# Attention and mixture of experts in fp32 on one core: sums of w1 kept in memory between two Strassen blocks, sums of w2 on GpSimd one visit ahead

## The chip, the cores and the metric

One core of a Trainium2 chip runs the whole kernel. The metric is device time in microseconds (us); lower is better. The engines are named as the profile names them: PE is TensorE (matmuls; PEld its weight loads), DVE is VectorE, ACT is ScalarE, POOL is GpSimd, SP is SyncE, which here issues nearly all transfers. SBUF is the on-chip memory that all engines read and write, PSUM the one that PE writes.

## The reference, cut to what matters

```python
def attention(q, k, v, omega):            # 4 batches, 8 heads, 576 tokens, 64 columns
    def phi(x): h = x @ omega.T - sum(x*x)/2; return exp(h - max(h)) / sqrt(128)
    q_p, k_p = phi(q * D**-0.25), phi(k * D**-0.25)
    return (q_p @ (k_p.T @ v)) / (q_p @ sum(k_p) + 1e-6)

x = attention(...).transpose(0, 2, 1, 3).reshape(2304, 512)
p = domain_probs / domain_probs.sum(-1)
for e in range(4):                        # w1[e]: 512 x 1024, w2[e]: 1024 x 512
    out += p[:, e:e+1] * (maximum(x @ w1[e], 0) @ w2[e])
```

## The kernel before

Every expert is cut in two halves of its 1024 hidden columns, which gives eight (expert, half) pairs. A *visit* works on one pair for one stretch of token rows: it makes the hidden rows (product with w1, relu), then the output rows (product with w2, scaled by the probability and added into `acc`). Visits 0 to 10 take the first 512 rows, while the attention of the later rows is worked off in between. Visits 11 to 18 (`u == 1`, the first Strassen block) take the next 896 rows for each of the eight pairs, and visits 19 to 26 (`u == 2`, the second block) the last 896 rows for the same eight pairs in the same order. The function of both blocks is `fast`.

All products are fp32 split in two fp32r parts (names ending in h or a for the high part, l for the low part): ACT copies the high part, POOL subtracts it for the low part (`split`, lines 491 and 494), and PE multiplies high by high, high by low and low by high. The product with w1 is Strassen-like, with seven products (`p1` to `p7`) in place of eight. Three of them use quarters of w1 as they are (`w1ah`, `w1al`, made by `direct`) and four use sums of quarters (`w1sh`, `w1sl`): `add` forms those sums in place in the raw tile `w1r` (lines 587 to 590, four instructions for each of two tiles), and `summed` splits them. `sides(v + 1)` makes all this for the next visit in six steps, each taken by a `next(ready)`.

In visits 19 to 25 (`DEEP`) the product with w2 uses seven products as well (`sevens`). It needs sums of rows of the hidden tiles (`t1`, `t2`, `r11`, split into `t_hl`) and sums of w2: `w2_sides` forms them in the tile `w2f` (`sums_of`, lines 539 to 542, four instructions for each of two halves of w2) and splits them into `w2s`. It is driven by `prepare()` inside the same visit; only its first step runs at the end of the visit before.

Instructions stand on each engine in the order in which the code emits them; each engine works in that order and waits at semaphores. A deep visit on PE is: eleven products of `p1` to `p6` (line 797, 448 columns), two groups of the first seventh, `p7(1)`, the third group, `p3(1)`, `p4(1)`, and then the remaining sevenths (line 861, 256 columns): sums 5, block (1, 0), the plain outputs of the fourth tile (lines 639 to 641), sums 6, block (1, 1), sums 7 and the last one. Each group of sevenths goes into half of a PSUM bank that DVE's `gather` (line 656) has read before.

Buffers: two each of `w1r`, `w1ah`, `w1al`, `w1sh`, `w1sl`; three of `w2r`; four of `w2h` and `w2l`; one of `w2f`. SP issues the loads of `w1r` and `w2r` when the buffer that each replaces has been read.

Of the kernel before, what the change touches and what calls it, by code (L numbers as in the profile page):

```python
# [6 lines left out]
F32 = mybir.dt.float32  # L7
# [7 lines left out]
def attention_moe(ctx, tc, kT, qT, kd, qd, kn, qn, vn, omT, probs, w1, w2, out):  # L15
# [10 lines left out]
    nc = tc.nc  # L26
# [15 lines left out]
    att = ctx.enter_context(tc.tile_pool(name="att", bufs=2))  # L42
    moe = ctx.enter_context(tc.tile_pool(name="moe", bufs=1))
    xs = ctx.enter_context(tc.tile_pool(name="xs", bufs=1))
    psum = ctx.enter_context(tc.tile_pool(name="psum", bufs=8, space=bass.MemoryType.PSUM))

    raw_x = xs.tile([P, NP, RING], F32, tag="raw_x", name="raw_x")
# [485 lines left out]
    def w2_sides(v, B):  # L533

        def sums_of(f):
            S = att.tile([P, 2, DM], F32, tag="k", name="w2f", bufs=1)
            (b11, b12), (b21, b22) = ((raw[v, "w2", c][:, :H], raw[v, "w2", c][:, H:]) for c in (f, 2 + f))
            (s2, s3), (s4, s1) = ((S[:, i, :H], S[:, i, H:]) for i in range(2))
            nc.vector.tensor_tensor(s1, b12, b22, ALU.add)  # L539
            nc.vector.tensor_tensor(s2, s1, b11, ALU.subtract)  # L540
            nc.vector.tensor_tensor(s3, b11, b12, ALU.subtract)
            nc.vector.tensor_tensor(s4, b21, s2, ALU.subtract)
            return S

        def plain(c):
            W[v, "w2", c] = a, b = pair_of(("w2h", 512), ("w2l", 512))
            split(raw.pop((v, "w2", c)), a, b, nc.scalar, nc.gpsimd)
            load("w2")

        def summed(S, f, i):  # L550
            tags = (("kp", "kp"), ("qp", "qp"), ("qt", "qt"), ("qth1", "qtl1"))[2 * f + i]
            B[f, i] = a, b = tuple(att.tile([P, DM], F32R, tag=x, name="w2s", bufs=1 if f * i else 2) for x in tags)
            split(S[:, i], a, b, nc.scalar, nc.gpsimd)

        S = sums_of(0)
        yield
        plain(0)
        yield
        summed(S, 0, 0)
        yield  # L560
        summed(S, 0, 1)
        yield
        plain(2)
        yield
        S = sums_of(1)
        plain(1)
        yield
        summed(S, 1, 0)
        yield
        summed(S, 1, 1)  # L570
        yield
        plain(3)
        yield

    def sides(v):

        tiles = [raw.pop((v, "w1", i)) for i in range(2)]
        A, S = {}, {}

        def direct(i):  # L580
            A[i] = ah, al = pair_of(("w1ah", 3 * H), ("w1al", 3 * H))
            for r, cs in ((tiles[i][:, :2 * H], slice(0, 2 * H)), (tiles[i][:, 3 * H:], slice(2 * H, 3 * H))):
                split(r, ah[:, cs], al[:, cs], nc.scalar, nc.gpsimd)

        def add(i):
            r11, r12, r21, r22 = (tiles[i][:, j * H:(j + 1) * H] for j in range(4))
            nc.vector.tensor_tensor(r22, r21, r22, ALU.add)  # L587
            nc.vector.tensor_tensor(r21, r11, r21, ALU.subtract)  # L588
            nc.vector.tensor_tensor(r11, r22, r11, ALU.subtract)
            nc.vector.tensor_tensor(r12, r12, r11, ALU.subtract)  # L590

        def summed(i):
            S[i] = sh, sl = pair_of(("w1sh", 4 * H), ("w1sl", 4 * H))
            split(tiles[i], sh, sl, nc.scalar, nc.gpsimd)
            W[v, "w1", i] = {
                p: tuple(x[:, j * H:(j + 1) * H] for x in t)
                for t, at in ((A[i], (1, 2, 4)), (S[i], (6, 3, 7, 5)))
                for j, p in enumerate(at)
            }
            load("w1")  # L600

        direct(0)
        yield
        direct(1)
        yield
        add(0)
        yield
        summed(0)
        yield
        add(1)  # L610
        yield
        summed(1)
        yield

# [134 lines left out]
    def start_sides2(v):  # L749
        B = {}  # L750
        g = w2_sides(v, B)
        next(g)
        sides2[v] = B, g

    def fast(v):

        u, n = visits[v][0], BIG // 2
# [7 lines left out]
        if deep:  # L765
            if v == DEEP[0]:
                sevens_t.append(xs.tile([P, 7, 2, WT], F32R, tag="raw_x", name="t_hl"))
                start_sides2(v)
            B, ready2 = sides2.pop(v)
            T = {p: (sevens_t[0][:, i], sevens_t[0][:, i + 1]) for p, i in ((5, 0), (6, 2), (7, 4))}  # L770
            t1, t2 = (x.rearrange("p t c -> p (t c)")[:, :2 * WT].rearrange("p (k x) -> p k x", k=2) for x in (va, vb))
            r11 = att.tile([P, 2, WT], F32, tag="q", name="r11", bufs=1)

        def prepare():
            if deep:
                next(ready2, None)
            else:
                split_w2()

# [83 lines left out]
        def sevens():  # L863

            L, R, QS3 = slice(0, H), slice(H, DM), range(3)

            def block(g, j):
                return [tuple(x[:, j * FH * P:j * FH * P + WT] for x in hs[2 * g + f]) for f in range(2)]

            def sums_of(i):  # L870
                return [tuple(x[:, f] for x in T[i]) for f in range(2)]

            def weights(g, cs):
                return [tuple(x[:, cs] for x in W[v, "w2", 2 * g + f]) for f in range(2)]

            def mixed(i, cs):
                return [tuple(x[:, cs] for x in B[f, i]) for f in range(2)]

            X, Z = [], []
            for q in QS3[:2]:  # L880
                X.append(bank("g2"))
                seventh(q, X[q][:, L], block(0, 0), weights(0, L))
            p7(1)
            less(t2[:, 1], last_rows(P_[1]["p5"]), t1[:, 1])
            X.append(bank("g2"))
            seventh(2, X[2][:, L], block(0, 0), weights(0, L))
            p3(1)
            less(t2[:, 0], last_rows(P_[1]["u2"]), t1[:, 0])
            p4(1)
            nc.gpsimd.tensor_tensor(r11, t2, r11, ALU.subtract)  # L890
            nc.scalar.activation(T[6][0], t2, AF.Copy)
            less(t1[:, 1], first_rows(P_[1]["u"]), t2[:, 1])
            for q in QS3:
                gather(v, X[q][:, L], q, L)
            nc.vector.tensor_tensor(T[6][1], t2, f32(T[6][0]), ALU.subtract)
            less(t1[:, 0], first_rows(P_[1]["p1"]), t2[:, 0])
            next(ready, None)
            split(r11, *T[7], nc.scalar, nc.gpsimd)
            for f in range(2):
                split(t1[:, f], *(x[:, FH * P:] for x in hs[f]), nc.scalar, nc.gpsimd)  # L900
            next(ready, None)
            yield 1
            for q in QS3:
                seventh(q, X[q][:, R], sums_of(5), mixed(1, R), start=False)
            yield 1
            zs = []
            for q in QS3:
                if q < 2:
                    Z.append(bank("g2"))
                zs.append(Z[q // 2][:, q % 2 * H:(q % 2 + 1) * H])  # L910
                seventh(q, zs[q], block(1, 0), weights(1, L))
            for q in QS3:
                gather(v, zs[q], q, L)
            next(ready, None)
            yield 1
            ps = bank("g2")
            outputs(v, hs, ps, 3, range(FH))
            gather(v, ps, 3)
            next(ready, None)
            yield 1  # L920
            for q in QS3:
                seventh(q, X[q][:, L], sums_of(6), mixed(0, L), start=False)
                gather(v, X[q], 4 + q)
            yield 1
            next(ready, None)
            for q in QS3:
                seventh(q, X[q][:, R], block(1, 1), mixed(1, L), start=False)
                gather(v, X[q][:, R], 4 + q, L)
            next(ready, None)
            yield 1  # L930
            for q in QS3:
                seventh(q, X[q][:, L], sums_of(7), mixed(0, R), start=False)
                gather(v, X[q][:, L], 4 + q, R)
            if v + 1 in DEEP:
                start_sides2(v + 1)
            yield 1
            for q in QS3:
                seventh(q, X[q][:, L], [tuple(x[:, FH * P:] for x in hs[f]) for f in range(2)], weights(1, R), start=False)
                gather(v, X[q][:, L], q, R)
            for t in range(tiles):  # L940
                gathered(v, t)
            yield 1
# [29 lines left out]
        if deep:  # L972
            nc.scalar.activation(r11[:, 1], first_rows(P_[0]["u"]), AF.Relu)
            less(t1[:, 1], last_rows(P_[0]["p5"]), r11[:, 1])
            p6(1)
            split(t1, *T[5], nc.scalar, nc.gpsimd)
            yield from sevens()
            return
        prepare()
# [309 lines left out]
```

## Time and profile before

| what | value |
|---|---|
| runs shown, median | 994.41 us (992.71 to 996.43, 3 runs) |
| the profiled execution's own time | 998.48 us |
| its span, from first to last instruction | 996.4 us |
| PE busy | 925.0 us (93%), 5286 matmuls |
| DVE, ACT, POOL busy | 653.7, 488.5, 497.9 us |
| moved by DMA | 83.63 MB, read 77.99 MB, written 4.72 MB |

Busy times are sums over the span; an engine that is not the last to be waited for can be idle at no cost. So the table says only that PE is nearest to being full; where PE is not, the views by stretch and by wait say.

### The profile page before, as it was taken

Reading aid. Unit: us, or ns where it says so; the run is one execution under the profiler, and the core shown is the slowest. Engines: PE = TensorE matmul, PEld = TensorE weight load, DVE = VectorE, ACT = ScalarE, POOL = GpSimd, SP = SyncE. Lnnn points to the kernel's source line nnn. Section 1 sums busy time; section 2 is a strip of 40 time slices with the busy share of each in tenths; the row PEclk is TensorE's granted clock in tenths of the full one; section 3 lists DMA queues with packets and bytes.
Section 4 is the critical chain, followed back from the end, with each engine's and each line's share of the span. In section 5 each row is a group of like instructions: output and inputs, shape, how many; then the busy total and the mean of one; then the engine's idle time right before and its main releaser. Section 6 shows DMA issues by size and latency. Waiting matters only on the chain. (4 is left out here: it accounts for less than half of the span.)

```text
span 996.4 us, 14354 instructions
## 1 busy us (share of the span) xinstructions
PE 925.0 (93%) x5286; PEld 816.6 (82%) x5286; DVE 653.7 (66%) x1076; ACT 488.5 (49%) x1092; POOL 497.9 (50%) x387
## 2 busy tenths in 40 slices
PE   9999999999999999999999999797878787878898
PEld 9898888887888888888888888687868686877787
DVE  5654677775685564657657578777676777776753
ACT  6455776776744645354535535454343434343430
POOL 5664565655344443434433344566565656564630
PEclk9999999999899999999999999998999998999899
DMA  7654454534215231312321122311101111202001
GB/s 194 163 185 148 127 162 141 162 124 143 74 53 148 75 98 56 101 43 64 101 64 43 42 64 85 95 43 43 53 32 53 32 53 33 68 19 74 11 11 74
DMA packets 47365, 83.63 MB, mean 84 GB/s; under 512 B 8704, under 2 KB 17088, under 8 KB 47296
## 3 DMA queue, kind: packets, MB, share of 16 engines
q1 hardware_dynamic: 47056, 82.43, 27.2%
q8 instruction: 41, 0.67, 0.3%
q10 hardware_dynamic: 240, 0.30, 0.1%
q14 instruction: 28, 0.23, 0.1%
HBM read 77.99 MB, written 4.72 MB: 83 GB/s over the span
## 5 line engine op out<-in xcount | busy, mean ns | idle before, releaser
L494 POOL TENSOR_TENSOR w2l<-w2r,w2h 128x512 fp32r<-128x512 f32 x93 | 126.4, 1365 | 141.2 <-ACT w2h L491 113.6
L656 DVE SCALAR_TENSOR_TENSOR acc<-g,pr,acc 128x512 f32<-128x512 f32 (+1 forms) x207 | 121.5, 616 | 69.0 <-PE g L641 40.9
L494 POOL TENSOR_TENSOR w1sl<-w1r,w1sh 128x1024 fp32r<-128x1024 f32 (+1 forms) x59 | 112.7, 1911 | 102.6 <-ACT w1sh L491 91.6
L639 PE MATMUL g<-w2h,hh 128*128 128x512 f32 x368 | 147.4, 401 | 0.4 <-ACT hh L843 0.4
L641 PE MATMUL g<-w2h,hl 128*128 128x512 f32 x368 | 144.5, 393 | 0.0
L640 PE MATMUL g<-w2l,hh 128*128 128x512 f32 x368 | 144.2, 392 | 0.0
L494 POOL TENSOR_TENSOR w1al<-w1r,w1ah 128x256 fp32r<-128x256 f32 (+1 forms) x77 | 89.4, 1178 | 53.1 <-ACT w1ah L491 46.3
L814 DVE SCALAR_TENSOR_TENSOR hl<-sum,hh 128x448 fp32r<-128x448 f32 (+1 forms) x96 | 64.3, 670 | 69.6 <-ACT hh L813 69.6
L808 DVE TENSOR_TENSOR sum<-g,sum 128x448 f32<-128x448 f32 x96 | 59.5, 620 | 75.5 <-PE g L797 74.7
L813 ACT ACTIVATE hh<-sum 128x448 fp32r<-128x448 f32 (+1 forms) x96 | 50.8, 529 | 116.6 <-DVE sum L808 116.6
L797 PE MATMUL g<-xbh,w1sh 128*128 128x448 f32 x256 | 94.9, 371 | 3.2 <-ACT sum L803 3.2
L491 ACT ACTIVATE w1sh<-w1r 128x1024 fp32r<-128x1024 f32 (+1 forms) x59 | 51.0, 867 | 95.6 <-DVE w1r L590 95.5
L861 PE MATMUL g<-w2s,t_hl 128*128 128x256 f32 x378 | 64.9, 341 | 33.7 <-ACT w1ah L491 18.7
L797 PE MATMUL g<-xbl,w1sh 128*128 128x448 f32 x256 | 94.2, 368 | 0.0
L797 PE MATMUL g<-xbh,w1sl 128*128 128x448 f32 x256 | 94.0, 367 | 0.0
L861 PEld LDWEIGHTS g<-w2s,t_hl 128*128 128x128 f32 x378 | 61.5, 246 | 38.0 <-ACT w1ah L491 20.8
L803 ACT ACTIVATE sum<-g 128x448 f32<-128x448 f32 x96 | 51.6, 538 | 72.9 <-PE g L797 72.9
L797 PE MATMUL g<-xbh,w1ah 128*128 128x448 f32 x192 | 72.2, 376 | 15.8 <-DVE sum L808 15.8
L641 PEld LDWEIGHTS g<-w2h,hl 128*128 128x128 f32 x368 | 69.4, 188 | 16.2 <-DVE hl L844 0.7
L639 PEld LDWEIGHTS g<-w2h,hh 128*128 128x128 f32 x368 | 69.6, 189 | 14.4 <-ACT hh L843 0.8
L640 PEld LDWEIGHTS g<-w2l,hh 128*128 128x128 f32 x368 | 69.5, 189 | 12.3
L797 PE MATMUL g<-xbh,w1al 128*128 128x448 f32 x192 | 70.9, 369 | 0.0
(195 smaller groups left out, 2234.8 us busy)
## 6 DMA issues: line engine op xcount, KB each, us to landing
w1r<-in_w SPq DMA_DIRECT2D x54, 512.0 KB, 3.6
w2r<-in_w SPq DMA_DIRECT2D x108, 256.0 KB, 2.7
out<-acc SPq DMA_DIRECT2D x18, 256.0 KB, 2.5
va<-in_vn SPq DMA_DIRECT2D x14, 256.0 KB, 4.6
k<-in_kd SPq DMA_DIRECT2D x12, 288.0 KB, 3.2
k<-in_kn SPq DMA_DIRECT2D x12, 288.0 KB, 4.4
q<-in_qd SPq DMA_DIRECT2D x12, 288.0 KB, 4.4
q<-in_qn SPq DMA_DIRECT2D x12, 288.0 KB, 5.0
```

Of the source, the lines that this page charges most:

```text
L491: hi.activation(a, t, AF.Copy)
L494: lo.tensor_tensor(c, t, f32(a), ALU.subtract)
L639: nc.tensor.matmul(ps, ha[:, ts_], wa, start=(c == 0), stop=False)
L640: nc.tensor.matmul(ps, ha[:, ts_], wc, start=False, stop=False)
L641: nc.tensor.matmul(ps, hc[:, ts_], wa, start=False, stop=(c == FH - 1))
L656: nc.vector.scalar_tensor_tensor(acc[i][:, cs], ps, sc, acc[i][:, cs], ALU.mult, ALU.add)
L797: nc.tensor.matmul(ps, a[:, w], x[:, k], start=(start and k + at == 0), stop=(k == 1 and at == 2), skip_group_check=not start)
L803: nc.scalar.activation(t, P_[g][where], AF.Copy)
L808: nc.vector.tensor_tensor(t, P_[g][where], t, ALU.add)
L813: nc.scalar.activation(ha, t, AF.Relu)
L814: nc.vector.scalar_tensor_tensor(hc, t, 0.0, f32(ha), ALU.max, ALU.subtract)
L861: nc.tensor.matmul(to, x, w, start=(start and f + k == 0), stop=(f + k == 3), skip_group_check=not start)
```

## The change

In the first block every visit stores its four tiles of split sums of w1 (high and low part of two tiles, 512 KB each) to memory, at the visit's start, through SP (`keep_sides`). In the second block `sides` leaves out `add` and `summed`: the tiles are loaded back from there by four DMAs that POOL issues (`fetched`), behind the first `direct`. The raw tiles `w1r` are still loaded, for the three quarters that `direct` takes.

The four additions of each `sums_of` of w2 move from DVE to POOL. `w2_sides` has another order of steps, and it starts one visit ahead: the first `sums_of` is emitted before `sevens()`, and both plain parts of the first half and its two summed splits inside `sevens()` of the visit before; `prepare()` does the rest, with a list that says how many steps each call takes.

```diff
@@ w2_sides
-            nc.vector.tensor_tensor(s1, b12, b22, ALU.add)
-            nc.vector.tensor_tensor(s2, s1, b11, ALU.subtract)
-            nc.vector.tensor_tensor(s3, b11, b12, ALU.subtract)
-            nc.vector.tensor_tensor(s4, b21, s2, ALU.subtract)
+            nc.gpsimd.tensor_tensor(s1, b12, b22, ALU.add)
+            nc.gpsimd.tensor_tensor(s2, s1, b11, ALU.subtract)
+            nc.gpsimd.tensor_tensor(s4, b21, s2, ALU.subtract)
+            nc.gpsimd.tensor_tensor(s3, b11, b12, ALU.subtract)
...
+    def keep_sides(v):
+
+        for i in range(2):
+            kept[visits[v][1:3], i] = ts_ = tuple(
+                scratch.tile([P, 4 * H], F32, tag=f"s{visits[v][1:3]}{i}{x}", name="kept", bufs=1) for x in "hl"
+            )
+            for k, t in zip(ts_, made.pop((v, i))):
+                nc.sync.dma_start(k, f32(t))
...
+        def fetched(i):
+            S[i] = pair_of(("w1sh", 4 * H), ("w1sl", 4 * H))
+            for t, k in zip(S[i], kept[visits[v][1:3], i]):
+                nc.gpsimd.dma_start(t, k)
+
+        direct(0)
+        if visits[v][0] < 2:
+            yield
+        else:
             load("w1")
-
-        direct(0)
-        yield
+            fetched(0)
+            parts(0)
+            fetched(1)
+            yield
+            direct(1)
+            load("w1")
+            parts(1)
+            yield
+            return
         direct(1)
...
+            steps2 = [2, 1, 1, 1, 1, 1, 1, 1] if v == DEEP[0] else [1, 1, 1, 0, 0, 1, 1, 0]
...
+        if u == 1:
+            keep_sides(v)
+
         def prepare():
             if deep:
-                next(ready2, None)
+                for _ in range(steps2.pop(0)):
+                    next(ready2, None)
...
             gather(v, ps, 3)
-            next(ready, None)
+            on_sides2(v + 1)
+            on_sides2(v + 1)
             yield 1
...
-            if v + 1 in DEEP:
-                start_sides2(v + 1)
+            on_sides2(v + 1)
             yield 1
...
             split(t1, *T[5], nc.scalar, nc.gpsimd)
+            if v + 1 in DEEP:
+                start_sides2(v + 1)
             yield from sevens()
```

PE has the same instructions in the same order in both kernels. On the other engines the change shows at three places of each deep visit.

The first place is DVE in `sevens`, from the split of t2 (L895, in the change L941) to the gather before the last groups; `acc<-g` are gathers. Before:

```order
L895 TENSOR_TENSOR t_hl<-vb,t_hl 128x768
L781 SCALAR_TENSOR_TENSOR va<-sum,vb 128x384
L656 SCALAR_TENSOR_TENSOR acc<-g_7222,pr,acc 128x256 x2
L656 SCALAR_TENSOR_TENSOR acc<-g_7229,pr,acc 128x256
L587 TENSOR_TENSOR w1r<-w1r 128x256
L588 TENSOR_TENSOR w1r<-w1r 128x256
L589 TENSOR_TENSOR w1r<-w1r 128x256
L590 TENSOR_TENSOR w1r<-w1r 128x256
L656 SCALAR_TENSOR_TENSOR acc<-g_7249,pr,acc 128x512
```

and four gathers on, the same four additions of the second tile. In the change:

```order
L941 TENSOR_TENSOR t_hl<-vb,t_hl 128x768
L827 SCALAR_TENSOR_TENSOR va<-sum,vb 128x384
L693 SCALAR_TENSOR_TENSOR acc<-g_7281,pr,acc 128x256 x2
L693 SCALAR_TENSOR_TENSOR acc<-g_7288,pr,acc 128x256
L693 SCALAR_TENSOR_TENSOR acc<-g_7312,pr,acc 128x512
L693 SCALAR_TENSOR_TENSOR acc<-g_7184,pr,acc 128x512
```

Both sets of additions are gone from between the gathers.

The second place is DVE beside the products `p2` to `p7` of the same visit; `sum<-g` reads a product from PSUM. Before:

```order
L808 TENSOR_TENSOR sum<-g_6995,sum 128x448
L814 SCALAR_TENSOR_TENSOR hl<-sum,hh 128x448
L539 TENSOR_TENSOR w2f<-w2r 128x256
L540 TENSOR_TENSOR w2f<-w2f,w2r 128x256
L541 TENSOR_TENSOR w2f<-w2r 128x256
L542 TENSOR_TENSOR w2f<-w2r,w2f 128x256
L808 TENSOR_TENSOR sum<-g_7057,sum 128x448
L814 SCALAR_TENSOR_TENSOR hl<-sum,hh 128x448
```

In the change:

```order
L854 TENSOR_TENSOR sum<-g_7063,sum 128x448
L860 SCALAR_TENSOR_TENSOR hl<-sum,hh 128x448
L854 TENSOR_TENSOR sum<-g_7113,sum 128x448
L860 SCALAR_TENSOR_TENSOR hl<-sum,hh 128x448
L854 TENSOR_TENSOR sum<-g_7048,sum 128x448
```

The four additions for w2 no longer stand between the read of `p2` and that of the later products.

The third place is POOL around `p4(1)`, from the split of t1 (`t_hl<-va`) on; `r` is r11. Before:

```order
L494 TENSOR_TENSOR t_hl<-va,t_hl 128x768
L890 TENSOR_TENSOR r_7376<-vb,r_7376 128x768
L494 TENSOR_TENSOR w1al<-w1r,w1ah 128x512
L494 TENSOR_TENSOR w1al<-w1r,w1ah 128x256
L494 TENSOR_TENSOR t_hl<-r_7376,t_hl 128x768
L494 TENSOR_TENSOR hl<-va,hh 128x384 x2
L494 TENSOR_TENSOR w1al<-w1r,w1ah 128x512
L494 TENSOR_TENSOR w1al<-w1r,w1ah 128x256
L494 TENSOR_TENSOR w1sl<-w1r,w1sh 128x1024 x2
```

In the change:

```order
L495 TENSOR_TENSOR t_hl<-va,t_hl 128x768
L540 TENSOR_TENSOR w2f<-w2r 128x256
L541 TENSOR_TENSOR w2f<-w2f,w2r 128x256
L542 TENSOR_TENSOR w2f<-w2r,w2f 128x256
L543 TENSOR_TENSOR w2f<-w2r 128x256
L936 TENSOR_TENSOR r_7436<-vb,r_7436 128x768
L495 TENSOR_TENSOR w1al<-w1r,w1ah 128x512
L495 TENSOR_TENSOR w1al<-w1r,w1ah 128x256
L625 DMA w1sh<-kept 128x1024
L625 DMA w1sl<-kept 128x1024
L625 DMA w1sh<-kept 128x1024
L625 DMA w1sl<-kept 128x1024
```

Four additions now stand ahead of `r`, four DMA issues behind the first `w1al`, ahead of `t_hl<-r`; the two `w1sl` of 1024 columns are gone.

On SP the four stores `kept<-w1sh`, `kept<-w1sl` of a visit of the first block stand behind the loads of `w1r` of the visit before and ahead of the visit's four loads of `w2r`.

## Rows read from the trace of the kernel before

**Rows 1.** Busy time by stretch: length, each engine's busy us, granted PE clock, DMA.
```profile
540.00:590.00 50.00, 50.00 (x244) 44.03 (x244) 28.75 (x41) 21.44 (x42) 20.89 (x16) 1.00 0.19 59
741.07:789.33 48.26, 39.15 (x222) 36.11 (x222) 34.71 (x57) 18.59 (x36) 28.21 (x19) 0.93 0.15 44
```

**Rows 2.** What PE waited for from 600 us on: us, times, longest.
```profile
PE g L861 <- ACT w1ah L491: 18.7, 6, 3.1
PE g L797 <- DVE sum L808: 15.8, 7, 3.0
PE g L861 <- DVE acc L656: 15.2, 11, 2.0
PE g L861 <- DVE hl L844: 5.8, 5, 1.2
PE g L861 <- ACT acc L654: 4.0, 2, 2.8
```

**Rows 3.** Timeline of PE, 741 to 790 us: rows with idle time before them.
```profile
742.55 3.87 PE L861 MATMUL g<-w2s,t_hl 128*128 128x256 f32 x18 [3.12 <-ACT w1ah L491]
...
754.16 0.50 PE L861 MATMUL g<-w2s,hh 128*128 128x256 f32 x2 [0.69 <-DVE acc L656]
...
758.55 3.34 PE L861 MATMUL g<-w2s,t_hl 128*128 128x256 f32 x18 [2.00 <-DVE acc L656]
...
777.65 0.47 PE L797 MATMUL g<-xbh,w1ah 128*128 128x448 f32 x1 [2.14 <-DVE sum L808]
...
782.10 0.39 PE L861 MATMUL g<-w2h,hl 128*128 128x256 f32 x1 [1.16 <-DVE hl L844]
```

**Rows 4.** Busy time by stretch, two stretches behind the third stall (columns as 1).
```profile
711.80:715.10 3.30, 3.30 (x18) 3.30 (x17) 2.23 (x6) 0.00 (x0) 1.48 (x1) 0.50 0.19 47
...
950.75:954.05 3.30, 3.30 (x16) 3.30 (x17) 1.48 (x4) 0.42 (x1) 2.38 (x1) 0.50 0.00 0
```

**Rows 5.** Timeline of DVE, 741 to 776 us: additions and what stands behind.
```profile
755.34 1.30 DVE L587 TENSOR_TENSOR w1r<-w1r 128x256 f32<-128x256 f32 x1
...
757.93 1.26 DVE L656 SCALAR_TENSOR_TENSOR acc<-g,pr,acc 128x256 f32<-128x256 f32 x3
...
771.66 1.50 DVE L539 TENSOR_TENSOR w2f<-w2r 128x256 f32<-128x256 f32 x1 [1.66 <-POOL w2s L494]
...
775.18 0.61 DVE L808 TENSOR_TENSOR sum<-g,sum 128x448 f32<-128x448 f32 x1
```

**Rows 6.** Timeline of DVE and POOL, 783 to 790 us.
```profile
785.90 0.62 DVE L814 SCALAR_TENSOR_TENSOR hl<-sum,hh 128x448 fp32r<-128x448 f32 x1 [0.70 <-ACT hh L813]
...
788.72 0.55 DVE L781 SCALAR_TENSOR_TENSOR vb<-sum,va 128x384 f32<-128x384 f32 x1
...
789.41 1.83 POOL L890 TENSOR_TENSOR r<-vb,r 128x768 f32<-128x768 f32 x1 [3.43 <-DVE vb L781]
```

**Rows 7.** Timeline of DVE, 776 to 783 us, beside POOL's w2s.
```profile
778.94 1.34 DVE L781 SCALAR_TENSOR_TENSOR va<-sum,r 128x384 f32<-128x384 f32 x1
```

**Rows 8.** Groups of POOL by shape: busy us, mean ns of one.
```profile
L366 POOL TENSOR_TENSOR raw_x<-nu,dn 128x256 f32<-128x256 f32 x8 | 5.9, 736 | 13.0 <-ACT hh L630 5.4 <-DVE dn L364 3.9 <-ACT sum L491 3.7
```

**Rows 9.** Timeline of POOL, 741 to 763 us, behind the first stall.
```profile
742.95 2.70 POOL L494 TENSOR_TENSOR w1al<-w1r,w1ah 128x512 fp32r<-128x512 f32 x2
745.61 2.16 POOL L494 TENSOR_TENSOR t_hl<-r,t_hl 128x768 fp32r<-128x768 f32 x1
```

**Rows 10.** DMA: issues by line (KB, us to landing), an SP timeline, a busy stretch.
```profile
w1r<-in_w SPq DMA_DIRECT2D x54, 512.0 KB, 3.6
...
28.02 2.39 SPq L124 DMA_DIRECT2D q<-in_qT  x4
...
56.00:60.00 4.00, 4.00 (x35) 3.81 (x33) 2.04 (x8) 1.76 (x5) 2.56 (x2) 1.00 0.98 304
```

**Rows 11.** Timeline of POOL and ACT around visit 18's start, 581 to 598 us.
```profile
581.62 2.40 POOL L494 TENSOR_TENSOR w1sl<-w1r,w1sh 128x1024 fp32r<-128x1024 f32 x1 [2.89 <-ACT w1sh L491]
...
597.23 0.62 ACT L491 ACTIVATE w2h<-w2r 128x512 fp32r<-128x512 f32 x1
```

More of the change, by code (lines that the diff above doesn't have):

```diff
@@ L44, in attention_moe @@
     xs = ctx.enter_context(tc.tile_pool(name="xs", bufs=1))
+    scratch = ctx.enter_context(tc.tile_pool(name="scratch", bufs=1, space=bass.MemoryType.DRAM))
     psum = ctx.enter_context(tc.tile_pool(name="psum", bufs=8, space=bass.MemoryType.PSUM))
@@ L546, in plain @@
             W[v, "w2", c] = a, b = pair_of(("w2h", 512), ("w2l", 512))
-            split(raw.pop((v, "w2", c)), a, b, nc.scalar, nc.gpsimd)
-            load("w2")
+            split(raw[v, "w2", c], a, b, nc.scalar, nc.gpsimd)
         def summed(S, f, i):
@@ L557, in w2_sides @@
         plain(0)
+        load("w2")
+        yield
+        plain(1)
+        yield
+        summed(S, 0, 1)
         yield
@@ L560, in w2_sides @@
         yield
-        summed(S, 0, 1)
+        plain(2)
+        load("w2")
         yield
-        plain(2)
+        plain(3)
         yield
         S = sums_of(1)
-        plain(1)
+        load("w2")
+        load("w2")
+        yield
+        summed(S, 1, 1)
         yield
@@ L569, in w2_sides @@
         yield
-        summed(S, 1, 1)
-        yield
-        plain(3)
-        yield
+    made, kept = {}, {}
+    def keep_sides(v):
[5 more added lines that the diff above has]
+                nc.sync.dma_start(k, f32(t))
     def sides(v):
@@ L594, in summed, with parts @@
             split(tiles[i], sh, sl, nc.scalar, nc.gpsimd)
+            made[v, i] = S[i]
+            parts(i)
+            load("w1")
+        def parts(i):
             W[v, "w1", i] = {
@@ L599, in summed @@
             }
-            load("w1")
-        direct(0)
-        yield
+        def fetched(i):
[4 more added lines that the diff above has]
+        if visits[v][0] < 2:
+            yield
+        else:
+            load("w1")
+            fetched(0)
+            parts(0)
+            fetched(1)
+            yield
+            direct(1)
+            load("w1")
+            parts(1)
+            yield
+            return
         direct(1)
@@ L753, in start_sides2, with on_sides2 @@
         sides2[v] = B, g
+    def on_sides2(v):
+        if v in sides2:
+            next(sides2[v][1])
     def fast(v):
@@ L918, in sevens @@
             gather(v, ps, 3)
-            next(ready, None)
+            on_sides2(v + 1)
+            on_sides2(v + 1)
             yield 1
@@ L924, in sevens @@
             yield 1
-            next(ready, None)
             for q in QS3:
@@ L928, in sevens @@
                 gather(v, X[q][:, R], 4 + q, L)
-            next(ready, None)
+            on_sides2(v + 1)
             yield 1
@@ L933, in sevens @@
                 gather(v, X[q][:, L], 4 + q, R)
-            if v + 1 in DEEP:
-                start_sides2(v + 1)
+            on_sides2(v + 1)
             yield 1
```

## The prediction

> **What bounds the kernel now.** I read the stretches first, to see where PE is not full, then the waits of PE summed by what ended them, then the timeline of one deep visit to find the instruction that is really late, and last the rows of the engines that would get new work.
>
> In the first block PE is busy for the whole 50 us that the first of [rows 1] shows, at full clock, so no faster preparation can shorten it; it can only be disturbed. A deep visit (the second row) is different: it lasts 48.26 us, PE is busy 39.15 of them, and the mean granted clock is 0.93. The 9.1 us without PE lie in five waits, which [rows 3] show for one visit: 3.12 us ahead of sums 5, 0.69 ahead of block (1, 1), 2.00 ahead of sums 7, 2.14 ahead of a product of the next visit and 1.16 ahead of its first sevenths. I call them stalls 1 to 5. [Rows 2] give their sums over the kernel.
>
> What ends each, read from [rows 5] and [rows 6]:
> - Stalls 2 and 3 end with gathers of DVE. The second of them, at 757.93, comes straight behind the additions of w1 that began at 755.34: DVE spent 2.59 us on work that PE does not need for another 20 us.
> - Stall 4 ends with the read of a product at 775.18. Ahead of it stand four additions of w2, from 771.66 on, the first of which had waited 1.66 us for POOL.
> - Stall 5 ends behind DVE operations that ran slowly beside POOL's splits of w2: 1.34 us in [rows 7] for an operation that takes 0.55 in [rows 6].
> - Stall 1 is named a wait for ACT, but what comes last is DVE's gather behind a chain of reads, splits and sums of p7(1) on DVE and ACT. None of it is in the diff, so this stall stays.
>
> The clock is the second loss. [Rows 4] show two stretches right behind stall 3 at a granted 0.50, the 1.2 GHz level, after full speed (2.4 GHz) and a wait; there are five such stretches of about 3.4 us, and the two rows are the first and the last. PE runs without a gap there, so each costs half its length, 1.7 us. The mean of 0.93 in the second of [rows 1] says the same of a visit: 0.07 of 48.26 is 3.4 us, two such losses, one behind stall 3 and one behind stall 1.
>
> **The change part by part.** The sum is made against the profiled execution, 998.48 us, and is scaled to the median, 994.41, at the end.
>
> Taken away. The eight w1 additions and the eight of w2 leave DVE, so stalls 2 to 4 lose their cause, and stall 5 loses it too, since POOL no longer splits w2 there. By [rows 2] that is 15.8 us (DVE sum), 15.2 (DVE acc), 5.8 (DVE hl), and of the 4.0 on ACT acc the part that is not stall 1 of the first deep visit, 4.0 − 2.8 = 1.2: together 38.0 us. The 18.7 us on w1ah are stall 1 of the other visits and stay. Without stall 3 the clock should stay up there: 5 × 1.7 = 8.5 us. Gained: **46.5 us**. From below, a gather waits for its own matmuls as well, and some tenths of each wait may remain: with 0.3 us left in each of these 25 waits it would be 7.5 us less.
>
> Put on POOL, first part: four additions of w2 ahead of r. The nearest row is POOL's 128x256 subtraction, 736 ns [rows 8], so 2.94 us a visit. POOL is idle there, 3.43 us, waiting for DVE's vb at 788.72 [rows 6], so by length they fit. But that idle time is just when DVE works through the chain that ends stall 1, from 785.90 to 789.27, with operations that read two tiles of SBUF, and [rows 7] show such an operation at 1.34 in place of 0.55 beside POOL. The cost lies between zero (the additions fall into DVE's own waits for ACT) and their whole length, 2.94 us a visit. Walking the two lists against each other, with an operation that meets one of POOL's held until that ends, two of the four additions land in DVE's waits for ACT and two hold it, so that vb ends about 1.5 us late (2 × 0.74). I take that. Six visits, 19 to 24, prepare a successor this way: **9.0 us** given back, with 0 and 17.8 as bounds; stall 1 grows from 3.1 to about 4.6 us.
>
> A rule of the Trainium skill speaks against the change here. Its page "SBUF — State Buffer", section "Who interferes with whom", has VectorE and GpSimd share one pair of ports under an exclusive lock: a VectorE operation with two SBUF inputs and a GpSimd operation exclude each other for a whole instruction. The 1.34 against 0.55 agrees with a wait of one instruction. Taken strictly for all four additions, the rule gives the bound of 17.8 us, a time of 967.
>
> The first deep visit has no visit ahead that would prepare it, and all its w2 work for the first half stands on POOL at once. By the same rows that is four low parts, two sums' low parts and the four additions, more than 10 us where 2.94 are new, of which half fits beside other work: **1.5 us** late, from 0 to 2.94.
>
> Put on POOL, second part: four DMA issues a visit, behind the first w1al and ahead of t_hl<-r. No row shows what a DMA issue costs POOL. From below, SP issues four in 2.39 us, 0.6 each; from above, I take the time in which such a transfer lands, 3.6 us, as if POOL were held until then [rows 10]. What waits behind is t_hl<-r, which sums 7 need. In [rows 9] w1al ends at 745.65, 3.1 us after sums 5 begin, and t_hl<-r takes 2.16. Sums 7 begin 758.55 − 742.55 = 16.0 us after sums 5 [rows 3], 13.3 without stalls 2 and 3. So an issue costs nothing up to (13.3 − 3.1 − 2.2) / 4 = 2.0 us, and each us above that costs 4 us a visit, 28 us over seven visits. I take 1.2 us, double SP's, nearer to that row than to the landing: cost **nothing**. In return POOL is rid of two w1sl a visit of 2.4 us each, by the first of [rows 11].
>
> On this the Trainium skill's page "DMA: Bandwidth & Descriptors", section "Latency and other measured facts", puts the first byte at about 1 us from GpSimd and 0.6 from SP. No row here shows the former; as an estimate from that page the four would hold POOL 4 us, and the sum is the same.
>
> The fetched tiles have to be there for the first product with a sum of w1, about 20 us after sums 5 begin. Issued between 3 and 8 us after it, and landing 3.6 us later (twice that if the 2.1 MB share the queues with w1r and w2r), they are there by 15: 5 us of cover, nothing paid.
>
> The stores. In the first block SP issues four of 512 KB per visit ahead of the visit's loads of w2r. They cannot start until w1sl is done, 581.62 + 2.40 = 584.02 for visit 18 [rows 11]; 2.1 MB at the 304 GB/s that a busy stretch moved [rows 10] take 7 us, so w2r is loaded by about 592, and ACT first uses it at 597.23. Cover 5 us, cost nothing; with the cover gone each us would cost up to 8, as PE is full there.
>
> The sum: 998.5 − 46.5 + 9.0 + 1.5 = 962.5 us. The profile lies 4.07 us above the median, so **958 us** (0.963 of before). A steady deep visit should come to 48.3 − 6.0 − 1.7 + 1.5 = 42.1 us.
>
> **The rivals.**
> - *No collision.* If POOL's additions end before DVE reaches its chain, 9 us of the price vanish: 949. For it: DVE's list is shorter ahead of that place, and POOL's sums can start earlier. Against it: 1.34 us in [rows 7]. If beyond that the clock stayed up behind stall 1 as well (6 × 1.7), 939.
> - *Full collision, or POOL late.* All four additions hold DVE (967), or an issue takes about 2.5 us (972). For it: POOL is the engine that gets both new kinds of work.
> - *The change does not deliver.* If stores hold w2r up past its cover, say by 2.5 us in eight visits of the first block, where PE has no slack, or the fetched tiles land as much too late, 20 to 30 us come back: 978 to 988. For it: SP's queue is in order. Against it: DMA is at 59 GB/s there [rows 1].
> - *The other side: the issues hold POOL.* With 3.6 us each, the four take 14.4; t_hl<-r comes 3.1 + 14.4 + 2.2 − 13.3 = 6.4 us late in seven visits: 45 us given back, 1003 us. It breaks even at 3.3 us an issue and is slower by over 0.5% from about 3.5. The skill's page "SBUF — State Buffer", section "SBUF: two separate sides", speaks for it: a DMA from GpSimd has its descriptors written by GpSimd, which VectorE's port use can lock out. No run here shows that yet. Against it: DVE is idle for part of that stretch, since it waits for PE's groups.
>
> **How the numbers follow.** The forecast's own range, 948 to 968, has a chance of 0.50; no collision (below 948) 0.13; full collision or POOL late (968 to 978) 0.18; not delivered (978 to 993) 0.11; POOL held by the issues 0.08. From 940 to 982 about 0.18 is left out: the held POOL, most of the undelivered case and the case with the clock up everywhere. 0.5%, 5 us, is about what a measurement of this kernel can tell from no change. Faster by more than that: all of the first three cases and half of the fourth, 0.87. Slower: most of the last, 0.06. Between: 0.07.
>
> **What would show it.** Stalls 2 to 5 should be gone from the waits of PE, with no more half-clock stretch behind sums 7 and a visit near 42 us. Stall 1 should stand at about 4.6 us, with POOL's additions of w2 beside lengthened DVE operations. Each issue on POOL should take less than 2.0 us, and the first block should keep PE full. If the first block grows, it is the stores; if sums 7 wait for POOL's t_hl, it is the issues; if the products with sums wait for a DMA, it is the fetch.

## The result, and the profile after

The changed kernel takes 948.4 us (median, 947.31 to 950.36) beside 995.26 us for the kernel before: ratio 0.9535, 95% interval 0.9508 to 0.9561. The forecast was 958, with a range of 940 to 982. The profiled execution spans 947.4 us, 49.0 less than before; the sum had 36.0.

Where the time came from: stretches of the profile after, with the columns of [rows 1].

```profile
540.00:590.00 50.00, 50.00 (x245) 44.01 (x244) 28.68 (x41) 21.55 (x42) 20.85 (x16) 1.00 0.34 116
688.15:728.88 40.73, 36.51 (x222) 34.45 (x223) 24.19 (x41) 17.28 (x34) 31.02 (x30) 0.93 0.31 104
```

The first block is as it was, PE busy all 50 us, though DMA moves 116 GB/s there in place of 59. A deep visit has shrunk from 48.3 to 40.7 us. DVE is down from 34.7 to 24.2 us of it, POOL up from 28.2 to 31.0.

The waits of PE from 600 us on, to be held against [rows 2]:

```profile
PE g L907 <- ACT w1ah L492: 24.2, 6, 4.2
PE g L907 <- ACT acc L691: 4.2, 2, 4.0
PE g L907 <- ACT hh L889: 1.8, 1, 1.8
PE g L907 <- DVE hl L890: 0.2, 1, 0.2
```

Stalls 2 to 5 are gone, but for some tenths in the first deep visit. Stall 1 has grown from 3.1 to 4.2 us, and one wait of 1.8 us is new, in the first deep visit. The two engines beside stall 1, DVE first, then POOL, in their timelines from 681 to 695 us:

```profile
682.08 1.25 DVE L860 SCALAR_TENSOR_TENSOR hl<-sum,hh 128x448 fp32r<-128x448 f32 x1 [0.65 <-ACT hh L859]
683.26 1.09 DVE L827 SCALAR_TENSOR_TENSOR vb<-sum,va 128x384 f32<-128x384 f32 x1
...
685.52 0.62 DVE L860 SCALAR_TENSOR_TENSOR hl<-sum,hh 128x448 fp32r<-128x448 f32 x1 [0.64 <-ACT hh L859]
686.06 0.55 DVE L827 SCALAR_TENSOR_TENSOR vb<-sum,va 128x384 f32<-128x384 f32 x1
```

```profile
682.11 0.74 POOL L540 TENSOR_TENSOR w2f<-w2r 128x256 f32<-128x256 f32 x1
682.93 1.00 POOL L541 TENSOR_TENSOR w2f<-w2f,w2r 128x256 f32<-128x256 f32 x1
684.00 0.92 POOL L542 TENSOR_TENSOR w2f<-w2r,w2f 128x256 f32<-128x256 f32 x1
684.89 0.72 POOL L543 TENSOR_TENSOR w2f<-w2r 128x256 f32<-128x256 f32 x1
...
691.14 0.57 POOL L625 DMA_DIRECT2D w1sh<-kept  x1
```

The first hl and vb take 1.25 and 1.09 us; the same two operations two rows down, with POOL past its additions, take 0.62 and 0.55. That is 1.17 us, and stall 1 is 1.1 us longer. Two of POOL's four additions are longer as well, 1.00 and 0.92 for 0.74. A DMA issue holds POOL 0.57 us.

### The profile page after: what moved, and what is told of

Read it like the earlier page. It is cut to its first block, busy times and chain, and to the rows that moved or that the text cites. A ratio compares the mean times of both kernels' runs of the same rounds, so it can differ in the third digit from the quotient of the medians.

```text
span 947.4 us, 14345 instructions
## 1 busy us (share of the span) xinstructions
PE 906.0 (96%) x5286; PEld 804.1 (85%) x5286; DVE 574.4 (61%) x956; ACT 476.2 (50%) x1076; POOL 518.3 (55%) x459
## 5 line engine op out<-in xcount | busy, mean ns | idle before, releaser
L495 POOL TENSOR_TENSOR w2l<-w2r,w2h 128x512 fp32r<-128x512 f32 x93 | 122.4, 1325 | 141.3 <-ACT w2h L492 107.3
L693 DVE SCALAR_TENSOR_TENSOR acc<-g,pr,acc 128x512 f32<-128x512 f32 (+1 forms) x207 | 124.4, 618 | 89.6 <-PE g L678 57.0
L495 POOL TENSOR_TENSOR w1al<-w1r,w1ah 128x256 fp32r<-128x256 f32 (+1 forms) x77 | 87.2, 1151 | 50.1 <-ACT w1ah L492 47.1
L495 POOL TENSOR_TENSOR w1sl<-w1r,w1sh 128x512 fp32r<-128x512 f32 (+1 forms) x43 | 74.9, 1743 | 61.0 <-ACT w1sh L492 52.7
L860 DVE SCALAR_TENSOR_TENSOR hl<-sum,hh 128x448 fp32r<-128x448 f32 (+1 forms) x96 | 59.4, 618 | 73.0 <-ACT hh L859 73.0
L907 PE MATMUL g<-w2s,t_hl 128*128 128x256 f32 x378 | 57.4, 314 | 28.1 <-ACT w1ah L492 24.2
L907 PEld LDWEIGHTS g<-w2s,t_hl 128*128 128x128 f32 x378 | 54.8, 219 | 31.1 <-ACT w1ah L492 26.3
L843 PE MATMUL g<-xbl,w1ah 128*128 128x448 f32 x192 | 70.1, 365 | 0.0
```

The costliest lines, as they stand in the source:

```text
L495: lo.tensor_tensor(c, t, f32(a), ALU.subtract)
L693: nc.vector.scalar_tensor_tensor(acc[i][:, cs], ps, sc, acc[i][:, cs], ALU.mult, ALU.add)
L843: nc.tensor.matmul(ps, a[:, w], x[:, k], start=(start and k + at == 0), stop=(k == 1 and at == 2), skip_group_check=not start)
L860: nc.vector.scalar_tensor_tensor(hc, t, 0.0, f32(ha), ALU.max, ALU.subtract)
L907: nc.tensor.matmul(to, x, w, start=(start and f + k == 0), stop=(f + k == 3), skip_group_check=not start)
```

## The experiments

Each ratio is to the kernel before, run on the same chip. The diffs are against the changed kernel where nothing else is said.

**1. The w1 part alone.** The w2 functions are those of before; the rest is the change.

```diff
-            nc.gpsimd.tensor_tensor(s1, b12, b22, ALU.add)
...
+            nc.vector.tensor_tensor(s1, b12, b22, ALU.add)
...
-            on_sides2(v + 1)
+            if v + 1 in DEEP:
+                start_sides2(v + 1)
```

> The w1 part alone: tiles of split sums stored in the first block and fetched in the second; the additions of w2 stay on DVE, inside their own visit, as before. Theory (each part takes away its own waits): the waits of PE on DVE's gathers (15.2 us and 1.2 us before) go, each with some 0.27 us that the idle rows don't show, and with them the half-clock stretches behind sums 7 (8.5 us); the waits on the product read (15.8 us) and on hl (5.8 us) stay, stall 1 stays at 3.1 us. Span 996.4 - 16.4 - 3.0 - 8.5 = 968 us, ratio to before about 0.972. Rival 1 (one late chain: taking DVE's w1 additions away only makes PE wait longer at the w2 additions): little gain, ratio 0.985 or more. Rival 2 (the w2 additions were late only because POOL was busy with w1sl): the waits on the product read and on hl go too, ratio near 0.95.

Measured: 964.04 us, 0.9685 (0.966 to 0.9709). The waits of PE from 600 us on:

```profile
PE g L901 <- ACT w1ah L492: 18.7, 6, 3.1
PE g L837 <- DVE sum L848: 15.0, 7, 2.2
PE g L901 <- ACT acc L687: 2.8, 1, 2.8
PE g L901 <- DVE hl L884: 2.3, 2, 1.2
```

The theory holds row by row: the gathers' waits are gone, stall 4 and stall 1 stand as in [rows 2]. Rival 2 has a small share, since hl fell from 5.8 to 2.3 us.

**2. The w2 part alone.** The w1 functions are those of before.

```diff
-        if visits[v][0] < 2:
-            yield
-        else:
-            load("w1")
-            fetched(0)
...
-            return
+        yield
...
-            keep_sides(v)
```

> The w2 part alone: additions of w2 on POOL, one visit ahead; the sums of w1 are formed on DVE and split on POOL in every visit, as before. Theory (each part its own waits): the waits on the product read (15.8 us) and on hl (5.8 us) go, with 0.27 us each that no idle row shows (3.2 us), the gathers' waits (16.4 us) and the clock loss behind sums 7 stay, and stall 1 grows by 1.1 us in six visits beside POOL's additions (6.6 us, and 1.2 us in the first deep visit). Span 996.4 - 24.8 + 7.8 = 979 us, ratio about 0.983. Rival (POOL, which keeps two w1sl of 2.4 us each and gets the additions, becomes late): PE waits for POOL's w2s or w2l about 3 us a visit, ratio 1.00 or more.

Measured: 995.0 us, 1.000 (0.9984 to 1.0017): nothing. The rival's number came out, but not by the rival's mechanism. The waits of PE, and DVE's second set of w1 additions with the POOL rows beside it:

```profile
PE g L872 <- ACT w1ah L492: 23.8, 6, 4.2
PE g L872 <- DVE acc L661: 22.1, 7, 3.9
```

```profile
706.28 1.30 DVE L592 TENSOR_TENSOR w1r<-w1r 128x256 f32<-128x256 f32 x1
707.61 1.37 DVE L593 TENSOR_TENSOR w1r<-w1r 128x256 f32<-128x256 f32 x1
709.01 1.37 DVE L594 TENSOR_TENSOR w1r<-w1r 128x256 f32<-128x256 f32 x1
710.41 0.42 DVE L595 TENSOR_TENSOR w1r<-w1r 128x256 f32<-128x256 f32 x1
710.76 1.26 DVE L661 SCALAR_TENSOR_TENSOR acc<-g,pr,acc 128x256 f32<-128x256 f32 x3
```

```profile
704.89 2.40 POOL L495 TENSOR_TENSOR w1sl<-w1r,w1sh 128x1024 fp32r<-128x1024 f32 x1 [2.37 <-ACT w1sh L492]
707.25 2.84 POOL L495 TENSOR_TENSOR w2l<-w2r,w2h 128x512 fp32r<-128x512 f32 x2
```

Stalls 4 and 5 went, as expected. But the two w2l that this part takes one visit ahead land beside DVE's second additions of w1 and stretch the second and third of them to 1.37 us, where an undisturbed one takes 0.42. (The first, 1.30 us, stands beside w1sl and took as long in the kernel before, in [rows 5].) The gather behind them comes 1.9 us later and stall 3 is 3.9 us. Stall 1 pays its 1.1 us too, and a stretch behind it of 5.45 us ran at half clock (741.45 to 746.90, granted 0.50). What the part saves at one end of the visit it loses at the other: PE's waits from 600 us on sum to 56.7 us in place of 61.2, and the mean granted clock, 0.959 in place of 0.968, takes the rest.

**3. The same, with the low parts of w2 back inside the visit** (diff against 2).

```diff
-            steps2 = [2, 1, 1, 1, 1, 1, 1, 1] if v == DEEP[0] else [1, 1, 1, 0, 0, 1, 1, 0]
+            steps2 = [2, 1, 1, 1, 1, 1, 1, 1]
...
-            on_sides2(v + 1)
-            on_sides2(v + 1)
...
```

> The w2 part alone, with the low parts of w2 back inside their own visit: POOL still makes the additions of w2 one visit ahead, but splits none of w2 beside DVE's additions of w1. Theory (the w2 part alone gained nothing because POOL's two w2l, moved one visit ahead, run beside DVE's second four additions of w1 and lengthen three of them from 0.43 to 1.37 us, which takes stall 3 from 2.0 to 3.9 us and prolongs the half clock behind it): stall 3 is back at 2.0 us, 6 x (1.9 + up to 1.7) = 11 to 21 us better than the w2 part alone, ratio to before 0.979 to 0.989. Rival 1 (stall 3 grew for another reason): it stays at 3.9 us, ratio 1.00. Rival 2 (POOL's low parts, back in the visit, are late there): new waits of PE for w2s or w2l take the gain, ratio 0.995 or more with stall 3 at 2.0.

Measured: 994.31 us, 1.001 (0.9993 to 1.0027). Rows of PE's waits, and ACT's timeline ahead of one of the second kind:

```profile
PE g L872 <- DVE acc L661: 15.1, 11, 2.0
PE g L872 <- ACT hh L854: 14.0, 7, 3.6
```

```profile
729.09 0.63 ACT L492 ACTIVATE w2s<-w2f 128x512 fp32r<-128x512 f32 x1 [2.83 <-POOL w2f L542]
```

The cause is confirmed: stall 3 is back at 2.0 us. (The text above counts three lengthened additions; the rows show two, as said in 2.) And rival 2 took the gain: with nine of the ten steps inside the visit POOL is late with its second set of additions, ACT's split of them waits 2.83 us, and the hh that the first sevenths need stands behind that split. PE waits 1.8 us for it in nearly every visit, 14.0 in all. So in these two runs the w2 part either starts early and meets the additions of w1 on DVE, or starts late and makes POOL late.

**4. POOL's additions behind r.**

```diff
             nc.gpsimd.tensor_tensor(r11, t2, r11, ALU.subtract)
+            if v + 1 in DEEP:
+                start_sides2(v + 1)
...
-            if v + 1 in DEEP:
-                start_sides2(v + 1)
             yield from sevens()
```

> The changed kernel with one place moved: the four additions of w2 for the next visit stand behind r on POOL, not ahead of it. Theory (the additions lengthen DVE's hl and vb beside them, 1.25 and 1.09 us for 0.62 and 0.55): those two go back to 0.62 and 0.55 us, stall 1 from 4.23 to 3.1 us in six visits, span 947.4 - 6.7 = 941 us, ratio to before 0.945 to 0.948. Rival 1 (stall 1 grew because POOL's r came late, or for another reason than the two operations): stall 1 stays at 4.2 us and the time at 948. Rival 2 (behind r the additions make POOL's later work late): stall 1 is 3.1 us, but PE waits for t_hl or w2s, time 948 or more.

Measured: 945.43 us, 0.950 (0.9473 to 0.9528), over the theory's 0.945 to 0.948 and with an interval that overlaps the changed kernel's. The mechanism is clear all the same, from the waits and DVE's timeline:

```profile
PE g L907 <- ACT w1ah L492: 18.3, 6, 3.1
```

```profile
683.32 0.62 DVE L860 SCALAR_TENSOR_TENSOR hl<-sum,hh 128x448 fp32r<-128x448 f32 x1 [0.65 <-ACT hh L859]
683.87 0.55 DVE L827 SCALAR_TENSOR_TENSOR vb<-sum,va 128x384 f32<-128x384 f32 x1
```

hl and vb are back at 0.62 and 0.55, stall 1 is 3.1 us, and PE's waits sum to 23.4 us in place of 30.4 in the changed kernel. The profiled execution (949.39 us, the longest of its runs) shows where they went: PE is busy 911.8 us in place of 906.0 for the same matmuls, at a mean granted clock of 0.976 in place of 0.982. Two visits of it, and what lies right behind stall 1 in each:

```profile
688.23:728.85 40.62, 37.56 (x223) 35.51 (x223) 22.48 (x41) 17.28 (x34) 30.53 (x30) 0.92 0.31 104
808.97:848.55 39.58, 36.52 (x223) 34.47 (x223) 22.48 (x41) 17.28 (x34) 30.57 (x30) 0.94 0.33 107
688.30:693.90 5.60, 5.60 (x26) 5.60 (x27) 2.83 (x4) 2.70 (x6) 5.44 (x7) 0.50 0.02 4
809.10:813.40 4.30, 4.30 (x25) 4.30 (x26) 2.78 (x4) 2.37 (x6) 4.14 (x6) 0.61 0.00 0
813.50:817.00 3.50, 3.50 (x23) 3.13 (x22) 1.27 (x3) 1.38 (x3) 3.50 (x6) 1.00 0.25 42
```

Behind one and the same stall the half clock went on for over 5.6 us in one visit and ended within 4.3 in the other; the visits differ by the 1.04 us that PE was busier. The six runs, 941.06 to 949.39 us, follow their mean clock, 0.985 to 0.976. At like clocks they are some 4 us shorter than the changed kernel's: 945.93 us at 0.981 and 944.93 at 0.982, beside 950.36 and 949.2.

**5. The gathers that end stall 1, earlier on DVE.**

```diff
             nc.scalar.activation(ha, t, AF.Relu)
+            for ps, q in between:
+                gather(v, ps, q, slice(0, H))
             nc.vector.scalar_tensor_tensor(hc, t, 0.0, f32(ha), ALU.max, ALU.subtract)
...
-            p7(1)
+            p7(1, [(X[q][:, L], q) for q in QS3[:2]])
...
-            p3(1)
+            p3(1, [(X[2][:, L], 2)])
...
-            for q in QS3:
-                gather(v, X[q][:, L], q, L)
```

> The changed kernel with the three gathers that end stall 1 earlier in DVE's order: those of X0 and X1 between the sum and the hl of p7(1), that of X2 between the sum and the hl of p3(1), where DVE waits 0.65 us for ACT. Theory (stall 1 is PE's wait for these gathers, whatever operation the wait row names): sums 5 follow p4(1) at once; the next wait is block (1, 0) for the hl of p4(1), about 1 us. 3.2 us a visit in seven visits, and up to 1.7 us a visit if the half-clock stretch behind the stall goes with it: span 914 to 925 us, ratio to before 0.92 to 0.93. Rival (stall 1 is a wait for ACT's w1ah or the chain behind r, as the row names it): no change, 947 us.

Measured: 917.22 us, 0.922 (0.9195 to 0.9244), the best version here. All waits of PE from 600 us on, and a deep visit:

```profile
PE g L909 <- DVE hl L892: 3.0, 6, 0.6
PE g L909 <- ACT hh L891: 1.8, 1, 1.8
PE g L909 <- ACT acc L691: 1.1, 1, 1.1
```

```profile
719.81:755.90 36.09, 35.39 (x222) 33.21 (x223) 26.42 (x41) 17.05 (x34) 32.06 (x30) 1.00 0.36 117
```

Stall 1 was PE's wait for these three gathers, though the wait row names ACT's w1ah. Without it the clock stays up in steady visits, and PE is busy 35.39 of 36.09 us.

**6. Those early gathers in the kernel before.** The edit of 5, on the kernel before.

> The kernel before, with nothing but the three gathers earlier in DVE's order as in the kernel with the early gathers. Theory (stall 1 is a fault of DVE's order that the change didn't touch and that stands beside its gains): stall 1 goes (18.7 and 2.8 us, 0.27 us each that no row shows, and the half-clock stretches behind it, up to 1.7 us each in seven visits), the waits on the product read, on later gathers and on hl stay: 996.4 - 23.4 - 12 = 961 to 973 us, ratio 0.965 to 0.978. Rival (only with a DVE freed of additions can the gathers come early): under 10 us, ratio over 0.99.

Measured: 984.62 us, 0.9906 (0.9877 to 0.9935): near the rival's bound, and far from the theory's 961 to 973. Waits of PE, and DVE's gathers ahead of one of the longest:

```profile
PE g L863 <- DVE acc L656: 29.4, 12, 4.6
PE g L797 <- DVE sum L808: 15.8, 7, 3.0
```

```profile
749.69 2.71 DVE L656 SCALAR_TENSOR_TENSOR acc<-g,pr,acc 128x512 f32<-128x512 f32 x4
```

Stall 1 is gone, and stall 2, 0.69 us before, is now 4.6: PE comes 3 us sooner to gathers that still stand behind the additions of w1 (744.48 to 749.77 us in this visit; the stall ends at 751.14). Stall 3 has shrunk from 2.0 us to under 0.5 in return. The same edit is worth 9 us there and 31 in the changed kernel (948.4 - 917.2).

**7. POOL's additions still later, in the version of 5.**

```diff
                 split(t1[:, f], *(x[:, FH * P:] for x in hs[f]), nc.scalar, nc.gpsimd)
+            if v + 1 in DEEP:
+                start_sides2(v + 1)
             yield 1
...
-            if v + 1 in DEEP:
-                start_sides2(v + 1)
             yield from sevens()
```

> The kernel with the early gathers, and in it POOL's four additions of w2 for the next visit moved behind its hl<-va, out of the way of DVE's hl of p4(1). Theory (what is left of stall 1, 0.64 us in five visits and 0.31 in one, is DVE late by the operations that POOL lengthens, and nothing else on POOL gets late by 2.9 us): those waits go, with 0.16 us each that no idle row shows, 3.0 + 1.0 us: span 912 us, ratio to before 0.918 to 0.92. Rival (POOL's later low parts come late): PE waits for w2s, w2l or w1al, 916 us or more.

Measured: 928.36 us, 0.9338 (0.9309 to 0.9366), 11 us worse than 5. The theory failed: hl still waits (2.7 us), and a new wait came. Of PE's waits, and ACT's timeline ahead of one:

```profile
PE g L843 <- ACT sum L849: 9.7, 6, 2.6
```

```profile
735.10 0.62 ACT L492 ACTIVATE w2h<-w2r 128x512 fp32r<-128x512 f32 x1
740.86 0.63 ACT L492 ACTIVATE w2h<-w2r 128x512 fp32r<-128x512 f32 x1 [5.13 <-DMA w2r<-in_w]
741.39 0.52 ACT L849 ACTIVATE sum<-g 128x448 f32<-128x448 f32 x1
```

ACT waits 5.13 us for a load of w2r, and the read of a product stands behind that split. POOL's w2l, 2.9 us of additions later than in 5, are what frees the raw tile for the load: SP issues it at 736.50 us, right behind the first of two w2l that run 2.54 us from 735.18. The trace shows this link; no edit tried it.

**8. Sixteen issues on POOL for four.**

```diff
-                nc.gpsimd.dma_start(t, k)
+                for j in range(4):
+                    nc.gpsimd.dma_start(t[:, j * H:(j + 1) * H], k[:, j * H:(j + 1) * H])
```

> The changed kernel with each of its four fetches of a visit cut into four transfers of 128x256 (128 KB): 16 issues on POOL in place of 4. Theory (an issue holds POOL 0.56 us whatever its size, as the four of the changed kernel do, and what is queued behind has a slack of (13.3 - 3.1 - 2.2) = 8.0 us): 16 x 0.56 = 9.0 us, t_hl<-r comes about 1 us later than sums 7 want it, and PE waits for it or for the low parts behind it 1 to 3 us a visit in seven visits: 955 to 970 us, ratio to before 0.96 to 0.975. Rival 1 (an issue costs by its bytes): 16 issues take 2.2 us as the 4 did, 948 us, ratio 0.953. Rival 2 (the low parts for w2 behind have much less slack): 5 us a visit or more, over 980 us.

Measured: 961.61 us, 0.9686 (0.9651 to 0.972). POOL's timeline and PE's wait:

```profile
696.48 2.13 POOL L626 DMA_DIRECT2D w1sh<-kept  x4
```

```profile
PE g L908 <- POOL t_hl L495: 4.0, 5, 1.0
```

Four issues of 128 KB take 2.13 us, as four of 512 KB do, so the price is by issue. Sixteen go just past the slack of 8 us: PE waits up to 1.0 us for t_hl, the wait that the prediction named. The 4.0 us are a third of the 13 lost. Of the rest, 1.2 us are further waits for hl (1.4 in place of 0.2) and 6.5 are PE's busy time (912.5 in place of 906.0), of which the clock (mean 0.980 in place of 0.982) holds some 2; it was not followed further.

## Why the prediction was right, and where it was off

- **The waits taken away** (38.0 us) came as worked out, and the wait of 1.7 us that was left out of the sum went as well. The parts don't add up, though: alone w1 gives 31 us and w2 nothing (1 and 2), together 47. The prediction's sum treated each stall as the property of its own edit; experiments 2 and 6 show that the stalls of a visit are linked through DVE's one queue, so that time taken from one comes back at the next, and 3 that POOL's queue can make such a link too.
- **The clock, and the price of a stall, is the term that was mis-sized.** The sum had 8.5 us for PE's busy time; it fell by 19.0, from 925.0 to 906.0. Two things were missing. The half clock was counted only behind stall 3: mean clock times span gives (1 - 0.968) x 996.4 = 31.9 us lost before and (1 - 0.982) x 947.4 = 17.1 after, 14.8 less (this counts the half clock inside waits too). The profile before has two more such stretches, behind stall 4 of the first two deep visits, with the columns of [rows 1]:

```profile
636.70:640.00 3.30, 3.30 (x10) 2.94 (x9) 3.27 (x4) 1.66 (x5) 2.86 (x2) 0.50 0.02 5
681.10:684.40 3.30, 3.25 (x9) 2.91 (x10) 2.89 (x4) 2.41 (x6) 3.04 (x3) 0.50 0.00 0
```

  They hold 2 x 1.7 = 3.4 us and went with stall 4: the granted clock after is 1.00 from 600 to 640 us and from 651.6 to 689. The other 3 of the 14.8 are not shown to be the change's doing; a part is a stretch ahead of both blocks, at 0.50 from 251.00 to 257.70 us before and shorter after. And a stall costs more than its idle row. In PE's timeline after, ahead of stall 1:

```profile
683.35 0.36 PE L843 MATMUL g<-xbl,w1ah 128*128 128x448 f32 x1
683.55 0.37 PE L843 MATMUL g<-xbh,w1al 128*128 128x448 f32 x1
688.15 2.15 PE L907 MATMUL g<-w2s,t_hl 128*128 128x256 f32 x12 [4.23 <-ACT w1ah L492]
```

  Matmuls start 0.20 us apart, so the next was due at 683.75 and came at 688.15, 4.40 us late, where the row says 4.23: the 0.17 by which a matmul outlasts its spacing count as busy. With 32 waits before and 10 after that is 3.7 us, and some tenths more, since the first matmul behind a stall is slow too.
- **The collision on POOL** (9.0 us, bounds 0 and 17.8) was the right mechanism: 1.1 us a visit in place of 1.5, 6.7 us in all, in 4 shown by undoing it. The walk had two additions holding DVE, which is what the rows show; each held it for 0.63 and 0.54 us, less than the 0.74 of a whole addition. The Trainium skill's page "SBUF — State Buffer", section "Who interferes with whom", agrees with the trace in which operations pay, hl and vb with two inputs in SBUF. Its strict bound of four whole instructions did not come, since DVE sat in waits for ACT and in a read of PSUM for the rest.
- **The first deep visit** (1.5 us) shows one wait of 1.8 and one of 0.2.
- **The issues** were taken at 1.2 us and free below 2.0: 0.57 us, and free. Experiment 8 bears out the slack of 8 us within about 1 us. The held POOL is refuted.
- **Stores and fetch** cost nothing: the first block is as full as before, and PE never waits for a fetched tile. The prediction's 592 for w2r left 1 us for w2r's own 1 MB, which is too little at its 304 GB/s; the stores did move SP's loads of it in visit 18 from 586.39 to 588.37 us, and the cover held that. The landings took 5.8 to 6.7 us by the page, not 3.6, which the cover still held:

```profile
kept<-w1sh SPq DMA_DIRECT2D x16, 512.0 KB, 5.8
...
w1sl<-kept POOLq DMA_DIRECT2D x16, 512.0 KB, 6.7
```

- **Stall 1 stays** was right, and so was its cause (5). The forecast visit of 42.1 us measured 40.7.
- **Two small sums** are off without consequence: the rows that should go hold 24 waits, not 25, and four additions of 736 ns in six visits are 17.7 us, not 17.8.

So the direction and the links were right; the 13 us by which the sum fell short (49.0 against 36.0) are 10.5 of PE's busy time and 2 to 3 of waits.

## What to carry to other kernels

Stalls that one engine's queue feeds are one chain: taking work out of it pays only where nothing else is late next, and the same edit can be worth 9 us or 31 depending on what else was taken out. When PE stalls, price the stall by the start times around it and look at the granted clock behind it; the idle row alone was too low here. And when a wait row names an operation whose result the waiting matmul doesn't read (here w1ah, for a matmul of w2s and t_hl), look for the operation that frees its PSUM bank: moving three gathers gave 31 us more.

## What the runs showed of the hardware that was not expected

- A DMA issue on POOL takes 0.55 to 0.57 us (medians, 0.53 to 0.73 over all) whether it moves 128 or 512 KB. On SP in the same execution the loads of w1r, 512 KB, took 0.33 us, and the stores to kept 0.64 and 0.83.
- The half clock behind one and the same stall lasted for over 5.6 us in one visit and under 4.3 in another of one execution. The runs of experiment 4, which lie 8 us apart, go with their mean clock.
- DVE and POOL both lose when they meet: beside DVE's two-input operations, POOL's additions took 1.00 and 0.92 us in place of 0.74. Beside two w2l of POOL, 2.84 us together, two DVE additions took 1.37 us each in place of 0.42 (experiment 2).
